# Giving one batch's feature sums a place of their own in the TensorE order, moving two GpSimd products to VectorE, and storing the last rows in two transfers instead of four

## The chip, the cores and the metric

The kernel runs on one core of a Trainium2 chip. Five engines work from instruction lists of their own: TensorE (PE in the profile; PEld is its weight loads), VectorE (DVE), ScalarE (ACT), GpSimd (POOL) and SyncE (SP, which here only issues transfers). An engine takes its list strictly in order, and waits at an instruction until the semaphores that it names have been raised by others. The metric is the device time of the program in microseconds, as the median of several runs. Before the change it is 265.54 us over 11 runs, from 265.09 to 267.2.

## The reference: what is computed

The first half is an attention without softmax over 4 batches, 4 heads, 1088 tokens and 32 channels per head. Every key and query is turned into 64 features, all products of two 8-number sketches:

```python
def phi(x):
    a = np.einsum('rd,bhsd->bhsr', S1, x)
    b = np.einsum('rd,bhsd->bhsr', S2, x)
    return np.einsum('bhsi,bhsj->bhsij', a, b).reshape(*x.shape[:-1], r * r)
q_p, k_p = (phi(q), phi(k))
kv = np.einsum('bhsf,bhsd->bhfd', k_p, v)
z = np.sum(k_p, axis=2)
num = np.einsum('bhsf,bhfd->bhsd', q_p, kv)
den = np.einsum('bhsf,bhf->bhs', q_p, z)[..., None] + 1e-06
return (num / den)
```

So each batch and head needs a 64 x 32 matrix `kv` and a vector `z` of 64 sums before its queries can be answered. The second half takes the 4352 rows of 128 numbers through `gelu(x @ w_in) @ w_out`, with 2048 hidden channels. The weights come as 64-bit floats; the kernel rounds them to 32 bits itself, out of their two 32-bit words.

## The kernel before, in words

**Tiles.** A batch's 1088 tokens are 1024 "main" tokens, worked in two chunks of 512 (eight chunks, n = 0 to 7), and 64 "remainder" tokens. The remainders of the four batches are chunk 8, of 256 tokens. The remainder's keys are worked in pairs: batches 0 and 2, and batches 1 and 3.

**The start.** Batch 0 is worked straight through, written out line by line from line 842. Keys are turned by TensorE, sketched, multiplied into features (line 383 by VectorE, line 380 by GpSimd) and multiplied with the values (`kv_first`, line 415). `key_features_rem(0, ..., by_pool=True)` (line 869) makes the remainder's features: ScalarE copies both sketches to SBUF (line 397) and GpSimd multiplies them (line 398). `kv_first_rem` (line 421) needs these; then ScalarE copies `kv` out (line 879), and the queries of chunk 0 are answered (line 625), divided (lines 640 to 646), turned (line 654) and given to the first hidden products (lines 688 and 673). Beside this the first two pieces of `w_in`, 256 columns each, are rounded (`class Rounding`): ScalarE scales the low words (line 260), VectorE takes the exponent field (line 264) and the mantissa field (line 266), ScalarE shifts the exponent (line 272), VectorE joins mantissa (line 280) and sign (line 285), and the last product (line 290) is GpSimd's for these two pieces. After the first of them GpSimd writes the gates of the `w_out` loads (line 180), and SyncE starts all further loads.

**The steps.** From line 911 on, the order is a list of steps t. Each step has one hidden product of 128 channels for a chunk (`hidden`, line 673), its GELU on ScalarE (line 680), then whatever was hung at that step with `at(t, ...)`, and then products with `w_out` (`project`, line 809, in the first steps; `two_products`, line 758, afterwards). Every instruction is tied to the one before it on its engine, so the order on each engine is the order of this text. Hidden results have two PSUM buffers.

**Batch 1's keys** (steps 14 to 23). VectorE turns the keys (line 352), spreads the features (lines 933 to 940), multiplies the remainder's (line 402), and adds over the tokens (`add_tokens`, lines 949 to 955), which leaves `k_s`, the partial sums for z. `finish_keys(1)` at step 21 does `kv_sum` on TensorE: 32 products for `kv` and 4 for its remainder (line 426), and then 4 products of `k_s` with ones for z, into the same PSUM bank beside `kv` (`part` 1). ScalarE copies 128 columns (line 444). At step 22 `turn_kv` turns `kv` (line 449), ScalarE copies it to `kz` (line 450), and VectorE folds z into the sketch of the queries (`sketch_of_z`, lines 475 to 478). `query_sketch(2)` at step 24 (line 560) needs that. Batches 2 and 3 go the same way at steps 45/46 and 77/78.

**The end.** Chunk 8's attention output is copied by ScalarE into `xT` (line 613), the two batches of a half side by side; two half results come from line 806, each for 128 tokens of two batches. `store` copies each to SBUF (line 815) and issues two transfers of 64 rows for it, one from SyncE's queue and one from ScalarE's (line 817).

## Time and profile before

| What | us |
|---|---|
| median of 11 runs | 265.54 |
| the profiled execution's own time | 265.54 |
| its span, first to last instruction | 263.8 |
| what lies around the span | 1.74 |
| TensorE busy in the span | 257.3 |
| VectorE, ScalarE, GpSimd busy | 150.5, 116.8, 165.9 |

The profiled execution has the time of the median, so sums made against it need no correction. "Busy" of TensorE counts a pipelined matmul to its modelled end. In the timeline each row gives start, duration, engine, line, operation, output and inputs, the count, and in brackets how long the engine was idle before it and who released it. Rows of one line are merged while they follow each other. The waits view has the same idle times summed: us in total, number, longest. TensorE's granted clock is at full speed in all stages before the last 2 us.

### The profile page before, as it was taken

The page shows a single profiled execution, that of the slowest core. Times are in us where ns is not written, and L with a number is a line of the kernel's source. Part 1 is how long each engine was busy: PE and PEld are TensorE (multiplying, and loading weights), DVE is VectorE, ACT ScalarE, POOL GpSimd, SP SyncE. Part 2 cuts the span into 40 slices and gives each one's busy share as a digit, 9 for nine tenths or more (in the row PEclk, how much of TensorE's full clock was granted, in tenths as well). Part 3 has the DMA queues.
Part 4 walks back from the last instruction along what each step waited for, and adds up shares of the span by engine and source line. Part 5 has one row for each costly group of instructions (what it writes and reads, how often), then busy time and mean ns, then how long its engine had stood idle before and what let it go on. Part 6 is the DMA issues. An engine that isn't in the chain of part 4 may idle for free.

```text
span 263.8 us, 5751 instructions
## 1 busy us (share of the span) xinstructions
PE 257.3 (98%) x2329; PEld 132.4 (50%) x2329; DVE 150.5 (57%) x305; ACT 116.8 (44%) x227; POOL 165.9 (63%) x175
## 2 busy tenths in 40 slices
PE   8999999979999999999999999999999999999994
PEld 6745444335454554444444454444445444445794
DVE  2886888958697996682176967560555032600240
ACT  4674777423625343353335333623453334433441
POOL 3614016779978775687767867777768776877200
PEclk9999999999999999999999999999999999999998
DMA  7479748710000201102000011001000100010020
GB/s 206 131 217 365 179 106 207 218 31 10 0 2 11 32 0 26 18 2 40 2 0 2 0 18 25 2 13 27 2 0 14 30 4 0 10 32 0 2 40 20
DMA packets 29562, 13.48 MB, mean 51 GB/s; under 512 B 21856, under 2 KB 27744, under 8 KB 29536
## 3 DMA queue, kind: packets, MB, share of 16 engines
q1 hardware_dynamic: 29344, 13.05, 19.8%
q8 instruction: 18, 0.29, 0.5%
q10 hardware_dynamic: 192, 0.07, 0.1%
q14 instruction: 8, 0.07, 0.1%
HBM read 10.88 MB, written 2.23 MB: 50 GB/s over the span
## 4 chain that ended last, share of the span: by engine, by line
PE 81%; DVE 6%; DMA 5%; SPq 5%; issue 1%; POOL 0%; ACT 0%; DVEq 0%
PE h_ps L673 37%; PE o_ps L758 33%; DMA block<-in_moe_w_out_dram 4%; PE w_ps L806 3%; DVE w_ps L949 1%; PE w_ps L609 1%; SPq L121 1%; PE w_ps L840 1%; SPq L132 1%; PE w_ps L560 1%; SPq L173 1%; PE w_ps L426 1%; DMA k<-in_k_dram 1%; DVE k_p L940 1%; PE h_ps L326 1%
## 5 line engine op out<-in xcount | busy, mean ns | idle before, releaser
L673 PE MATMUL h_ps<-xT,w_in 128*64 128x512 f32 (+3 forms) x516 | 138.7, 576 | 0.0
L680 ACT ACTIVATE block<-h_ps 128x512 f32<-128x512 f32 (+1 forms) x128 | 73.0, 570 | 120.7 <-PE h_ps L673 114.2
L758 PE MATMUL o_ps<-block,w_out 128*64 128x256 f32 x224 | 57.7, 380 | 0.0
L673 PEld LDWEIGHTS h_ps<-xT,w_in 128*64 128x64 f32 (+1 forms) x516 | 42.1, 143 | 30.1 <-issue 11.7
L723 POOL TENSOR_TENSOR bits_low<-block 128x512 f32<-128x512 f32 x28 | 35.6, 1273 | 29.8 <-ACT block L680 29.8
L758 PEld LDWEIGHTS o_ps<-block,w_out 128*64 128x64 f32 x224 | 30.2, 137 | 38.5 <-issue 25.8
L724 POOL TENSOR_TENSOR bits_a<-block 128x512 f32<-128x512 f32 x28 | 35.8, 1280 | 13.9 <-ACT block L680 13.9
L725 POOL TENSOR_TENSOR bits_e<-bits_a,block 128x512 f32<-128x512 f32 x28 | 36.2, 1294 | 2.2
L726 POOL TENSOR_TENSOR bits_m<-block,bits_e 128x512 f32<-128x512 f32 x28 | 35.8, 1279 | 2.2
L758 PE MATMUL o_ps<-block,small 128*64 128x256 f32 x112 | 29.1, 382 | 0.0
L758 PE MATMUL o_ps<-bits_low,small 128*64 128x256 f32 x112 | 29.1, 382 | 0.0
L758 PE MATMUL o_ps<-bits_a,small 128*64 128x256 f32 x112 | 29.0, 381 | 0.0
L774 DVE TENSOR_TENSOR sums<-o_ps,sums 64x512 f32<-64x512 f32 x8 | 5.5, 683 | 41.2 <-ACT sums L771 23.6
L758 PE MATMUL o_ps<-bits_m,w_out 128*64 128x256 f32 x112 | 28.7, 379 | 0.0
L572 DVE STREAM_TRANSPOSE w_ps<-w_ps 128x512 f32<-128x512 f32 (+1 forms) x7 | 4.8, 691 | 39.6 <-PE w_ps L560 39.6
L758 PEld LDWEIGHTS o_ps<-block,small 128*64 128x64 f32 x112 | 14.8, 137 | 19.0 <-issue 10.6
L758 PE MATMUL o_ps<-bits_e,small 128*64 128x256 f32 x112 | 17.1, 384 | 0.0
L809 PE MATMUL o_ps<-g,w_out 128*128 128x512 f32 x32 | 16.4, 600 | 0.1
L758 PEld LDWEIGHTS o_ps<-bits_m,w_out 128*64 128x64 f32 x112 | 15.3, 137 | 0.0
L758 PEld LDWEIGHTS o_ps<-bits_a,small 128*64 128x64 f32 x112 | 14.9, 137 | 0.0
L758 PEld LDWEIGHTS o_ps<-bits_low,small 128*64 128x64 f32 x112 | 14.8, 137 | 0.0
L758 PEld LDWEIGHTS o_ps<-bits_e,small 128*64 128x64 f32 x112 | 7.5, 136 | 10.6 <-issue 9.1
(181 smaller groups left out, 300.5 us busy)
## 6 DMA issues: line engine op xcount, KB each, us to landing
block<-in_moe_w_in_dram SPq DMA_DIRECT2D x3, 512.0 KB, 6.8
block<-in_moe_w_out_dram SPq DMA_DIRECT2D x3, 512.0 KB, 11.8
k<-in_k_dram SPq DMA_DIRECT2D x12, 128.0 KB, 2.7
v<-in_v_dram SPq DMA_DIRECT2D x12, 128.0 KB, 3.1
q<-in_q_dram SPq DMA_DIRECT2D x24, 64.0 KB, 2.1
out_dram<-oT SPq DMA_DIRECT2D x24, 64.0 KB, 2.2
k<-in_k_dram SPq DMA_DIRECT2D x2, 256.0 KB, 2.7
q<-in_q_dram SPq DMA_DIRECT2D x2, 256.0 KB, 3.8
```

The source lines that it names most:

```text
L121: sp.dma_start(out=q_sb[n][h * 32:(h + 1) * 32].rearrange("t x j d -> t (x j d)"), in_=q[n // NCH, h, at:at + CW, :].rearrange("(t n) d -> ...
L572: dve.transpose(out=tok, in_=ps[:, :, :H2])
L673: pe.matmul(ps[rows, :W], lhsT=w[:, rows], rhs=xT[n][:, :W], start=True, stop=True)
L680: act.activation(out=g_of[n, fi][:, :W], in_=ps[:, :W], func=ACT.Gelu)
L723: pool.tensor_sub(out=s[3], in0=a11, in1=a21)
L724: pool.tensor_add(out=s[1], in0=a21, in1=a22)
L725: pool.tensor_sub(out=s[2], in0=s[1], in1=a11)
L726: pool.tensor_sub(out=s[4], in0=a12, in1=s[2])
L758: pe.matmul(acc[n][bank][half * 64:(half + 1) * 64, col:col + HW], lhsT=fixed, rhs=moving, start=opens and e == 0 and name in "4715", stop ...
L774: dve.tensor_add(out=C[lo, 1], in0=a1[lo], in1=C[lo, 0])
L806: pe.matmul(o_of[n][i][:, :128], lhsT=g[:, i * 128:(i + 1) * 128], rhs=w_tile(w_out_sb, fi), start=first, stop=final)
L809: pe.matmul(o_of[n], lhsT=w_tile(w_out_sb, fi), rhs=g, start=first, stop=final)
```

## The change

Five edits.

1. `kv_sum` no longer does the four z products. A new `z_sum` does them, with a start of its own, and a new `fold_z` does the fold into the query sketch. For batch 1 the z products move from step 21 (right behind `kv`) to step 23, behind that step's hidden product; the fold moves from step 22 to step 23, behind them. For batches 2 and 3 the order on TensorE and VectorE stays as it was.
2. `take_kv` copies 64 columns and not 128.
3. The first remainder features (batches 0 and 2) are made as the second ones are: ScalarE copies one sketch, VectorE multiplies it with the other out of PSUM. They come ahead of the rounding of `w_in[0]` on VectorE, and GpSimd does nothing for them.
4. `w_in[1]`: its mantissa field (line 266) moves behind the divisions of chunk 0, and its last product moves from GpSimd to VectorE, ahead of the two products of `expand_multiply` (line 538).
5. Chunk 8's `xT` is written with the two batches of a half interleaved token by token (each ScalarE write steps over one element), so that a half's 128 rows go out in one transfer from SyncE; ScalarE issues none.

```diff
         def fields(self):
+            self.exponent_fields()
+            self.mantissa_fields()
...
-    def key_features_rem(pair, ps, by_pool=False):
+    def key_features_rem(pair, ps):
...
-        both = att.tile([128, H, 2 * R], FP, name="a_rem")
-        if by_pool:
-            act.copy(out=both, in_=ab)
-            pool.tensor_mul(**spread(k_p_rem[pair], both[:, :, 0:R], both[:, :, R:2 * R]))
-            return
-        a = both[:, :, 0:R]
+        a = att.tile([128, H, R], FP, name="a_rem")
         act.copy(out=a, in_=ab[:, :, 0:R])
         dve.tensor_mul(**spread(k_p_rem[pair], a, ab[:, :, R:2 * R]))
...
+    def z_sum(b):
+
+        ps = held["kv"][:, 0]
         for h in range(H):
-            kv_product(ps, ones, k_s[b][:, h], h, 1, stop=True)
+            kv_product(ps, ones, k_s[b][:, h], h, 1, start=True, stop=True)
+
+    def fold_z(b):
+        sketch_of_z(b, held["kv"][:, 0], F)
...
     def take_kv(b, ps):
-        kv_T[b] = att.tile([128, 128], FP, name="kv_T")
-        act.copy(out=kv_T[b], in_=ps[:, :128])
+        kv_T[b] = att.tile([128, F], FP, name="kv_T")
+        act.copy(out=kv_T[b], in_=ps[:, :F])
...
-            pe.matmul(banks[rows, 1, :128], lhsT=kv_T[b][:, :F], rhs=ident, start=True, stop=True)
+            pe.matmul(banks[rows, 1, :128], lhsT=kv_T[b], rhs=ident, start=True, stop=True)
         act.copy(out=kz[b], in_=banks[:, 1, :128])
-        sketch_of_z(b, banks[:, 0], F)
...
-        act.copy(out=xT[n][:, :W].rearrange("p (s x) -> p s x", s=2), in_=banks[:, :, :W // 2])
+        to = xT[n][:, :W]
+        to = to.rearrange("p (s x) -> p s x", s=2) if m == 1 else to.rearrange("p (s t i) -> p s i t", s=2, i=m)
+        act.copy(out=to, in_=banks[:, :, :W // 2] if m == 1 else banks[:, :, :W // 2].rearrange("p s (i t) -> p s i t", i=m))
...
-                for b, queue in ((i, sp), (i + 2, act)):
-                    queue.dma_start(out=out[b * S + MAIN:(b + 1) * S, :],
-                                    in_=oT[b // 2 * REM:(b // 2 + 1) * REM, i, :])
+                sp.dma_start(out=out.rearrange("(two b s) d -> two b s d", two=2, s=S)[:, i, MAIN:S, :].rearrange("two s d -> s two d"),
+                             in_=oT[:, i, :])
...
-    key_features_rem(0, banks[1], by_pool=True)
+    key_features_rem(0, banks[1])
...
-    w_in[1].fields()
+    w_in[1].exponent_fields()
...
     for banks, tokens in zip(nd, parts):
         divide(0, banks, tokens, by_head_pair=True)
+    w_in[1].mantissa_fields()
...
-    w_in[1].product(pool)
+    w_in[1].product()
...
-    def finish_keys(b):
+    def finish_keys(b, z=True):
         held["kv"] = work_banks()
         kv_sum(b, held["kv"][:, 0])
+        if z:
+            z_sum(b)
         take_kv(b, held["kv"][:, 0])
...
-    at(21, finish_keys, 1)
+    at(21, finish_keys, 1, False)
     at(22, lambda: turn_kv(1, held["kv"]))
+    at(23, z_sum, 1)
+    at(23, fold_z, 1)
     at(23, query_turn, 3)
...
             at(t + 14, lambda b=b: turn_kv(b, held["kv"]))
+            at(t + 14, fold_z, b)
```

## The prediction

> **What bounds the kernel now.** I first read the page's busy line: does one engine fill the span? TensorE does, with 257.3 of 263.8 us. What is left to win is therefore its own idle time, and the second view is the list of TensorE's waits over the whole span, longest first.

> ```profile
> PE 257.3 (98%) x2329; PEld 132.4 (50%) x2329; DVE 150.5 (57%) x305; ACT 116.8 (44%) x227; POOL 165.9 (63%) x175
> ```

> ```profile
> PE w_ps L426 <- DVE k_s L955: 1.6, 1, 1.6
> PE w_ps L840 <- PEq L1128: 0.8, 1, 0.8
> PE o_ps L421 <- POOL k_p_rem L398: 0.3, 1, 0.3
> PE h_ps L654 <- DVE x_tok L646: 0.2, 1, 0.2
> ```

> The whole list has four entries, and two are touched: the 1.6 us before batch 1's z products and the 0.3 us before the first remainder's. The third view is busy time by stage (columns: length, PE, PEld, DVE, ACT, POOL busy with counts, granted clock, DMA share, GB/s).

> ```profile
> 44.00:52.00 8.00, 8.00 (x43) 2.53 (x41) 7.90 (x10) 3.69 (x9) 6.62 (x10) 1.00 0.72 209
> 52.00:56.00 4.00, 2.42 (x86) 1.55 (x86) 2.83 (x3) 1.23 (x3) 3.25 (x3) 1.00 0.26 64
> 56.00:60.00 4.00, 4.00 (x42) 1.69 (x38) 1.34 (x4) 1.82 (x4) 2.94 (x3) 1.00 0.14 22
> 60.00:100.00 40.00, 40.00 (x388) 19.57 (x380) 34.81 (x59) 16.33 (x32) 32.63 (x37) 1.00 0.05 9
> ```

> VectorE fills 44 to 52 (7.90 of 8): it makes batch 1's keys, and TensorE runs into its end. Behind that, TensorE has no hole until the last 4 us, so a microsecond won at 53 is kept if nothing else turns late. Fourth, the timeline around the hole and around the start and end:

> ```profile
> 10.66 0.77 POOL L398 TENSOR_TENSOR k_p_rem<-a_rem 128x256 f32<-128x256 f32 x1 [0.82 <-ACT a_rem L397]
> 11.49 0.42 PE L421 MATMUL o_ps<-v_rem_aug,k_p_rem 128*64 128x33 f32 x8 [0.26 <-POOL k_p_rem L398]
> ...
> 17.59 0.30 PEld L673 LDWEIGHTS h_ps<-xT,w_in 128*128 128x128 f32 x2 [0.75 <-POOL w_in L290]
> ...
> 53.05 0.29 PE L426 MATMUL w_ps<-k_p_rem,v_rem_aug 128*32 128x64 f32 x8
> ...
> 54.46 0.42 DVE L955 TENSOR_TENSOR k_s<-w_ps,k_p_rem 64x256 f32<-64x256 f32 x1
> ...
> 54.93 0.32 PE L426 MATMUL w_ps<-k_s,ones 128*32 128x64 f32 x8 [1.58 <-DVE k_s L955]
> 55.18 1.08 PE L673 MATMUL h_ps<-xT,w_in 128*64 128x512 f32 x4
> ...
> 259.97 1.18 SPq L817 DMA_DIRECT2D out_dram<-oT  x2
> 259.97 1.44 ACTq L817 DMA_DIRECT2D out_dram<-oT  x2
> ```

> TensorE ends kv's remainder at 53.34, waits 1.58 for `k_s`, and two hidden products that need no `k_s` stand behind the wait.

> **Part 1, z at step 23.** After kv's remainder TensorE now goes on with step 22's hidden product. In the chain before, the hidden product behind small matmuls took 1.01, the turn of kv 0.22, the next hidden product 0.86: z comes up at 53.34 + 2.09 = 55.43. Two things must be ready. `k_s` ends at 54.88 and released TensorE at 54.93: 0.50 to spare. The new instruction also waits for ScalarE, up to the copy `kz`, which stands behind step 22's GELU; before, `kz` ended at 57.06, 1.88 after that hidden product began, so now at about 55.22: 0.2 to spare. ScalarE's own copy of kv no longer waits for z (53.34 instead of 55.25), and a hidden buffer is free, as step 21's GELU ended by 52.96. Behind z on TensorE stand step 23's `w_out` products and step 24's hidden product; a late z would hold them. z's eight records take 0.22 in batch 2, where they follow without a hole; the products behind them took 1.01 there where 0.86 is usual, so 0.15 goes back. Old start of those products: 57.33. New: 55.43 + 0.22 + 0.15 = 55.80, a gain of 1.53; the bare hole is 1.58. I take 1.55. Bounds: 1.85 without any refill time (hole, 0.10 less on z, 0.15 less on the hidden product, rounded up), 0.8 if z waits for a VectorE that slips by 1.2 (below).

> What is late next? The fold on VectorE took 57.09 to 57.85. It would now run from about 55.8 to 56.6; the query sketch (line 560) comes up at 55.80 + 1.30 + 0.86 = 57.96, so 1.3 to spare. The turn of chunk 3's queries behind the fold (0.71) moves along. GpSimd's sums of the next block waited 1.56 for a GELU at 56.98; they can now follow the previous ones at 55.41. Cost: nothing.

> **Part 2, the narrower copy.** 0.27 each, three times, shorter by some hundredths; TensorE has a hidden product (0.86) between copy and turn. Nothing, and nothing if that cover went.

> **Part 3, the first remainder features.** GpSimd's 0.77 goes. VectorE is free of `q_pT` at 10.54, and ScalarE's copy ends at 10.58. The same product on VectorE took 0.41 (line 402, same shape, one input from PSUM): about 10.62 to 11.03. TensorE ends `kv_first` at 11.23 and goes straight on: 0.26 won. The price lies behind it on VectorE: the fields of `w_in[0]`, formerly 10.46 to 10.96, start at about 11.03. ScalarE's line 272 waits for the first of them and stands ahead of the copy of kv (line 879): 11.03 + 0.29, then 0.50 is 11.85, then 0.22 is 12.07. TensorE has the query turns (0.57 up to the next start) after line 421 and wants kv at 12.18. So 0.1 to spare; if the product takes 0.7, the gain falls to 0.1. Line 285 ends at about 12.3, not 12.05, GpSimd's product of `w_in[0]` moves 0.24 later, and with it the gates on POOL's queue and every later load on SyncE's. Those have room: the 512 KB blocks of `w_out` landed in a median of 11.8, so the first, issued at 15.54, near 27.3, and VectorE read it at 28.73; GpSimd's copy of the remainder values ended 3.4 before its next work. On the other side VectorE loses what stood beside GpSimd: line 280 took 0.66 beside line 398 where 0.42 is usual, line 266 took 0.83 beside line 290 where 0.29 is usual.

> **Part 4, `w_in[1]`.** Line 266 leaves the stretch before the divisions and falls into VectorE's 0.59 hole before 15.64, where it fits with 0.29. The product needs 0.42 on VectorE (line 290 for `w_out[0]`) after line 285 and its 0.42, instead of 0.73 on GpSimd and a handover: ready at 17.15, not 17.54. The hidden product that needs it stood at 17.59, and the six records there took 2.92 where six steps of 0.43 are 2.58 and 0.16 is usual run-out: 0.18 was waiting. The next limit is the GELU that frees the buffer, so I take 0.10. `expand_multiply` moves to 18.1 from 17.92; its reader starts at 19.5, or 19.15 now. `w_out[0]` follows and is read at 20.2. Parts 3 and 4 together: 0.36, between -0.1 (all of it eaten, w_in[0] late) and 0.7 (the 0.2 of line 654 and the rest of the 0.3 also go).

> **Part 5, the end.** Before, the last two transfers were issued at 260.65; SyncE's issue took 0.51 to 0.53, ScalarE's 0.55 and 0.77; landing took 1.8 and 2.1 (medians). Now one of 64 KB from SyncE: 64 KB stores landed in a median of 2.2, 64 KB query loads in 2.1, with issues of 0.42 to 0.63. Against ScalarE's 0.77 and 2.1 I take 0.10 won, between 0.3 won (SyncE's 1.8 stays) and 0.9 lost (the slowest landing of any store, 3.0). The first transfer's issue ends before the second copy is done, so nothing queues. The interleaved copy (line 613) has 0.06 to spare before TensorE's hidden product at 241.94. The nearest row for a step of 8 bytes is line 260's reading, 0.43 against 0.37 for a plain 128x256 copy: 0.00 to 0.07, I take 0.03 lost.

> [...]

> **Sum.** 265.54 - 1.55 - 0.36 - 0.10 + 0.03 = 263.56; I say 263.5, as the bounds of parts 1 and 3 reach further down than the refill I charged.

> **Rivals.**
> - Only the middle pays (12 in 100): ScalarE's order eats the start, the end is even. 265.54 - 1.55 = 264.0. For it: 0.1 to spare at kv's copy. Against: VectorE gets back 0.78 of time lost beside GpSimd.
> - The wait comes back at z (10 in 100): VectorE's key stage is full, and 0.24 later loads or GpSimd's neighbourhood (line 285 took 0.94 at 44.67 against 0.69) may shift `k_s`. From 0.5 late on it costs; 1.2 late leaves 0.8 of part 1: 264.3. If nothing of it were won and the start paid: 265.1. Against: VectorE's chain there starts from ScalarE work that TensorE paces, so it moves forward with the start.
> - More than the sum (8 in 100): the start gives 0.7, the end 0.3, the refills vanish: 262.7.
> - Slower (4 in 100): VectorE becomes the bound between 60 and 103, where it is 87% busy. Its two-input sums took 0.41 or 1.42 (lines 792, 793) by what GpSimd did beside them, and the fold of batch 2 at 102.0 has 0.84 before TensorE's line 560 at 102.86. A shifted phase adds 1.0 per hit; it decides from 0.84 + 2.0 = 2.8 late, three hits. Four would give 263.5 + 4.0 - 0.84 = 266.7. Against: two of the three sums there are already the slow kind.
> - The forecast itself: 66 in 100, with a range of 263.1 to 263.9.

> **Range and chances.** 262.8 to 264.6 takes in the forecast, the middle alone, the wait half back and most of the better case; outside lie the slow case and parts of the others. A measurement of this kernel tells 0.2% (0.5 us) from no change. Faster: all but the slow case and the worst of the returning wait, 92; within 0.2%: 4; slower: 4.

> **What would show it.** Right: no TensorE wait for `k_s`, z products about 2.1 us after kv's remainder, line 560 of batch 1 some 1.9 earlier than 59.42; line 421 without a wait and near 11.23; no PEld wait for GpSimd's `w_in`; one SyncE issue per half and a similar tail after the last copy. Wrong: a wait of TensorE for ScalarE's kv copy near 12.2, for `kz` or `k_s` near 55, a new hole near 100, or a tail over 3.5 us from the last copy to the end.

## The result and the profile after

The changed kernel takes 264.22 us, the median of 15 runs (263.75 to 265.24), against 265.47 us over 57 runs of the kernel before on the same chip: a ratio of 0.9953, with a 95% interval of 0.9941 to 0.9964. That is 1.25 us less. The prediction was 263.5 us, 2.0 less than the profiled execution of before: the sign is right, the time lies inside the range, and about 0.7 us of the gain is missing. Of all executions told of here, one, of the kernel "early and one" below, ran in a slower state of the chip (272.01 us at a granted clock of 0.95), and it is left out of every comparison.

The profiled execution of the changed kernel took 265.24 us (span 263.5), the longest of its runs, so its span is not compared with the other; places in it are. First the busy line of its page and the list of TensorE's waits over the whole span (what it waited for, us in total, times, longest):

```profile
PE 257.6 (98%) x2329; PEld 132.5 (50%) x2329; DVE 151.2 (57%) x307; ACT 116.8 (44%) x227; POOL 163.5 (62%) x173
```

```profile
PE w_ps L849 <- PEq L1143: 0.8, 1, 0.8
PE h_ps L635 <- issue: 0.5, 1, 0.5
PE o_ps L819 <- DVE w_out L297: 0.5, 1, 0.5
PE o_ps L768 <- DVE sums L789: 0.3, 1, 0.3
PE h_ps L664 <- DVE x_tok L656: 0.2, 1, 0.2
```

The two entries that the prediction counted on are gone: the 1.6 for `k_s` and the 0.3 for the remainder's features. Three have come: 0.5 inside the 64 products of line 635 (the query answers, 625 before), 0.5 for VectorE's last product of the second `w_out` piece (297, 290 before), and 0.3 near 199 us for VectorE's sums. None was in the prediction.

The busy time by stage, in the columns and windows of the prediction:

```profile
44.00:52.00 8.00, 8.00 (x41) 2.72 (x42) 7.83 (x11) 3.94 (x8) 6.61 (x10) 1.00 0.75 207
52.00:56.00 4.00, 4.00 (x90) 1.95 (x88) 3.69 (x4) 2.51 (x6) 3.84 (x4) 1.00 0.32 88
56.00:60.00 4.00, 4.00 (x48) 1.87 (x48) 1.78 (x5) 1.23 (x3) 3.92 (x4) 1.00 0.12 19
60.00:100.00 40.00, 40.00 (x392) 19.56 (x390) 34.97 (x60) 16.59 (x32) 31.89 (x37) 1.00 0.06 10
```

From 52 to 56 TensorE is now busy for 4.00 of 4.00, where it was 2.42. Behind that nothing has opened up to 100. The timeline shows how (start, length, engine and line; line 428 is kv and z, 683 the hidden product, 458 kv's turn, 459 ScalarE's copy `kz`, 965 VectorE's last step of `k_s`):

```profile
53.92 0.29 PE L428 MATMUL w_ps<-k_p_rem,v_rem_aug 128*32 128x64 f32 x8
...
54.15 1.08 PE L683 MATMUL h_ps<-xT,w_in 128*64 128x512 f32 x4
...
55.06 0.39 PE L458 MATMUL w_ps<-ident,kv_T 128*64 128x128 f32 x4
...
55.36 0.42 DVE L965 TENSOR_TENSOR k_s<-w_ps,k_p_rem 64x256 f32<-64x256 f32 x1
55.77 0.26 ACT L459 COPY kz<-w_ps 128x128 f32<-128x128 f32 x1
56.23 0.16 PEld L428 LDWEIGHTS w_ps<-k_s,ones 128*32 128x32 f32 x8 [0.81 <-ACT kz L459]
56.24 0.32 PE L428 MATMUL w_ps<-k_s,ones 128*32 128x64 f32 x8
```

z comes 2.03 behind the end of kv's remainder (54.21), where 2.09 was worked out; `k_s` is ready at 55.78, 0.46 before z, where 0.50 was. `kz` ends at 56.03, 0.2 before z, as said. The weight loads' 0.81 idle before `kz` costs nothing, as the matmuls have no gap.

At the end there is one issue per half, the second copy goes on beside the first issue, and from the start of that copy to the end of the span it is 3.40 (before 3.44, from its copy at 260.32):

```profile
259.71 1.29 SPq L826 DMA_DIRECT2D out_dram<-oT  x2
260.06 0.29 DVE L825 COPY oT<-w_ps 128x128 f32<-128x128 f32 x1 [0.38 <-PE w_ps L816]
```

To put the whole together I timed TensorE's own list in stages, between the same instructions in every profile: from the first query products (the 16th record of line 534, 7.8 us in before) to the end. That leaves out how early the first loads came in: the start of the list lies between 7.43 and 7.96 in these five. Three more executions stand beside the two that are compared; they are told of below.

```
us from ... to                          before  after  again  one more  one fewer
query products .. tokens turned (664)     7.39   7.88   7.36      7.36       7.00
.. step 4's output products (819)         7.93   8.23   8.24      7.85       7.85
.. batch 1's query sketch (568)          36.32  34.81  34.81     34.81      34.81
.. 192 us                               132.71 132.71 132.71    132.71     132.72
.. 204 us                                11.90  12.26  12.26     11.91      11.91
.. last product                          55.96  55.98  55.96     55.98      55.98
.. end of the span                        3.75   3.71   3.72      3.71       3.71
```

The middle gives 1.51 in each of the four. The rest is a matter of three places: the first row, which varies; the second, 0.3 worse where 0.1 better was expected; and the row to 204, 0.35 worse.

### The profile page after: what moved, and what is told of

It is laid out like the page before. It is cut to its first block, busy times and chain, and to the rows that moved or that the text cites. A ratio compares the mean times of both kernels' runs of the same rounds, so it can differ in the third digit from the quotient of the medians.

```text
span 263.5 us, 5749 instructions
## 1 busy us (share of the span) xinstructions
PE 257.6 (98%) x2329; PEld 132.5 (50%) x2329; DVE 151.2 (57%) x307; ACT 116.8 (44%) x227; POOL 163.5 (62%) x173
## 4 chain that ended last, share of the span: by engine, by line
PE 93%; DVE 3%; issue 1%; POOL 1%; ACT 0%; DVEq 0%
PE h_ps L683 43%; PE o_ps L768 33%; PE o_ps L819 5%; PE w_ps L816 3%; PE w_ps L617 1%; PE w_ps L428 1%; PE w_ps L849 1%; PE w_ps L568 1%; PE o_ps L417 1%; PE h_ps L333 1%; PE w_ps L935 1%; DVE q_pT L546 0%; PE w_ps L534 0%; DVE x_tok L656 0%; PE h_ps L635 0%
## 5 line engine op out<-in xcount | busy, mean ns | idle before, releaser
L690 ACT ACTIVATE g<-h_ps 128x512 f32<-128x512 f32 x16 | 9.5, 596 | 7.7 <-PE h_ps L683 7.2
```

The source lines that it names most:

```text
L690: act.activation(out=g_of[n, fi][:, :W], in_=ps[:, :W], func=ACT.Gelu)
```

## The experiments

Each was run in five rounds beside the kernel before on the same chip, so each has its own ratio to it.

**First the parts.** At this point the profile after was all there was, and its largest new entry the stand inside line 635. Theory A: TensorE's own supply of instructions fails there now and then. Theory B: the new order makes that hole in every execution. Theory C: the gain of the middle is given back later. The changed kernel was run again, and three kernels with some of its parts. The edits are the diff of the change, cut into its parts:

```diff
 e1_again:      all of it
 e2_z_only:     parts 1 and 2 (z_sum, fold_z, the narrower kv_T)
 e3_start_only: parts 3 and 4 (key_features_rem on VectorE; w_in[1])
 e4_end_only:   part 5 (one transfer per half, the interleaved xT copy)
```

> The changed kernel once more, for a second profiled execution. In the first one TensorE was 0.19 us ahead at 12.25, then stood still inside the 64 products of line 635 until 13.37 with nothing that released it, and VectorE's last product for w_out[1] came 0.5 late at 23.42; the middle gave 1.50. Theory A (the stand-still is TensorE's own supply of instructions, which comes when it comes, and varies from execution to execution): the hole of line 635 is smaller or gone or elsewhere in this execution, the span is shorter by what it lost, and times between 263.7 and 265.2 again. Theory B (the new order itself makes it, in every execution): the same hole of 0.8 at the same place and the same late product at 23.4. Median against before: 0.994 to 0.997.

> Of the change only z_sum and fold_z at step 23 and the narrower copy. Start and end as before. Prediction's part 1: 1.5 us less than before (ratio 0.994, about 264.0), the hole at line 428 gone and z some 2.1 behind kv's remainder. Theory A: this alone is as fast as the whole change or a little faster, as the start edits give nothing. Theory C (the middle's gain is given back later, through a new wait near the drains): the ratio is 0.996 or more and TensorE has new waits behind 60.

> Only parts 3 and 4: first remainder features and w_in[1]'s product by VectorE, its mantissa field later. The prediction had 0.36 us less (ratio 0.9986). Theory A: no wait at the remainder's products, 0.2 ahead at 12.2, then some of it lost where TensorE runs out of instructions: ratio 0.998 to 1.001, with the hole before batch 1's z products still 1.5 to 1.9. Theory B: 0.4 to 0.8 us more than before (ratio 1.0015 to 1.003).

> Only part 5: interleaved xT, one transfer per half. The prediction had 0.07 us less. All theories: between 0.2 less and 0.3 more (ratio 0.999 to 1.001); the copy of xT in 0.37 to 0.44, the time from the last VectorE copy to the end 3.2 before, 3.0 to 3.3 here.

Measured: again 264.13 us (ratio 0.9957, 0.9943 to 0.9972); z alone 263.99 (0.9945, 0.9926 to 0.9965); the start alone 265.51 (1.0002, 0.9989 to 1.0015); the end alone 265.23 (1.0002, 0.9984 to 1.0021).

So z alone gives as much as the whole change, and the two start edits together give nothing. Theory B falls for the stand inside line 635, which is in neither of the two other profiles with the start edits, as theory A has it. C falls too: z alone keeps 1.4. The other half of B holds, the late product of `w_out[1]`: all three profiles so far with both start edits have 0.51 to 0.53 of waiting for line 297, and no profile without them shows it.

**What holds line 297?** In the profile after, five rows tell it:

```profile
22.49 0.41 DVE L292 SCALAR_TENSOR_TENSOR bits_e<-small,bits_r 128x256 uint32<-128x256 uint32 x1
...
22.87 0.60 PE L664 MATMUL w_ps<-ident,x_tok 128*128 128x128 f32 x4
...
23.14 0.24 POOL L476 TENSOR_TENSOR S_ab<-sT,own_r 128x32 f32<-128x32 f32 x1
...
23.42 0.42 DVE L297 TENSOR_TENSOR w_out<-bits_m,bits_e 128x256 f32<-128x256 f32 x1 [0.52 <-POOL S_ab L476]
...
23.99 1.10 PE L819 MATMUL o_ps<-g,w_out 128*128 128x512 f32 x2 [0.52 <-DVE w_out L297]
```

VectorE ends the signs (292) at 22.90 and stands idle for 0.52 with everything ready, while GpSimd works through the eight small instructions of `spread_sketches`. In before, signs and product stand close together, with the same instructions of GpSimd beside them:

```profile
22.01 0.41 DVE L285 SCALAR_TENSOR_TENSOR bits_e<-small,bits_r 128x256 uint32<-128x256 uint32 x1
22.53 0.45 DVE L290 TENSOR_TENSOR w_out<-bits_m,bits_e 128x256 f32<-128x256 f32 x1
```

In the changed kernel the profile names one of GpSimd's as the releaser. My theory D was that GpSimd's small instructions keep VectorE out. Two kernels try it, one by moving these instructions to 13 us, one also without part 4; and two take parts 3 and 4 alone:

```diff
 e5_early_spread (the changed kernel), e8_all_but_win (parts 1, 2, 3, 5)
     load_rest()
+    spread_sketches()
...
-    at(11, spread_sketches)
 e6_features_only: part 3 alone        e7_win_only: part 4 alone
```

> The changed kernel with GpSimd's eight small instructions of `spread_sketches` (own_r, S_abc, S_ab; 22.30 to 24.12 in its profile) issued right behind the gates of the last loads, so at about 13.3, where GpSimd stands idle for 8.31 us. Theory D (VectorE's last product for w_out[1], line 297, is locked out by these small instructions because the w_out chain comes 0.2 later by one more product on VectorE): VectorE's 0.52 idle before that product goes, TensorE's 0.5 before step 4's output products goes down to the 0.0 to 0.2 that ScalarE's copy of xT leaves, and the time is 0.3 to 0.5 below the changed kernel: 263.6 to 263.85, ratio to before 0.993 to 0.994. Rival E (that wait only covers another one of the same length, or GpSimd's instructions now hold VectorE up at 13 to 15 in the divisions): 264.1 to 264.4, the wait moves to another place before 25 us.

> Part 3 alone (the remainder's first key features by VectorE, w_in[1] left as before). Theory D: nothing is added to VectorE behind 12 us, so the w_out chain is not later, line 297 comes before GpSimd's small instructions as in the kernel before, and the gain at the remainder's products is kept: 0.2 to 0.3 less than before, 265.15 to 265.25, ratio 0.999. Rival F (the gain at 11 us is eaten before 23 us whatever stands there, by ScalarE or by the divisions): 265.4, ratio 1.000, with a new or longer wait of TensorE between 12 and 24.

> Part 4 alone (w_in[1]'s mantissa fields behind the divisions, its product on VectorE; the remainder's features on GpSimd as before). Theory D: the w_out chain on VectorE is some 0.2 to 0.3 later, line 297 of w_out[1] is locked out by GpSimd's small instructions, and TensorE waits 0.5 for it near 23.5: 0.3 to 0.5 slower than before, 265.75 to 265.95, ratio 1.0015. Rival F: the product is ready 0.3 to 0.4 earlier and nothing else moves: 265.3 to 265.45, ratio 0.9995 to 1.000.

> Parts 1, 2, 3 and 5 without part 4 (w_in[1] by GpSimd as before), and with `spread_sketches` at 13 us as in the run with it early. Theory D: the sum of what each part gives without the lock-out: the middle 1.45, the first features 0.25, the end 0.05 to 0.1, so 263.6 to 263.75, ratio 0.993 to 0.9935, below the changed kernel (264.15) and z alone (264.0). Rival F (the start gives nothing in any form): 263.9 to 264.0, as z and the end alone would.

Measured: early 263.68 (0.9928, 0.9907 to 0.9950); part 3 alone 265.56 (0.9996, 0.9975 to 1.0018); part 4 alone 265.33 (0.9997, 0.9974 to 1.0020); all but part 4 264.14 (0.9939, 0.9914 to 0.9964). The time of the first is what D foretold, and D is wrong all the same. The profile of that kernel has no GpSimd instruction between 21.1 and 22.0, and the stand is there, to the hundredth:

```profile
21.08 0.41 DVE L292 SCALAR_TENSOR_TENSOR bits_e<-small,bits_r 128x256 uint32<-128x256 uint32 x1
...
22.02 0.42 DVE L297 TENSOR_TENSOR w_out<-bits_m,bits_e 128x256 f32<-128x256 f32 x1 [0.52 <-DVE bits_e L292]
```

What had gone was the 0.3 near 199, 175 us after anything that the edit touches. D's other three numbers were missed too. Part 4 alone does not lock line 297 out, and part 3 alone gains nothing.

**Theory G: the place in the list.** I then numbered VectorE's instructions in each trace, its first one as number 0 and semaphore waits included (of the changed kernel's 378 records, 68 are such bare waits, 0.02 to 0.05 us each, which the timeline does not print; none of the other 310 names more than one semaphore). In all profiles so far I looked for instructions that start at least 0.25 us after VectorE was free and after everything they wait for was done. (Where `S_ab` is named as the releaser, this is what hides it: later GpSimd work raises the same semaphore again, but the product needs only GpSimd's sum of line 285, done at 22.35.) They are these:

```
kernel                     number   instruction                    idle   just ahead of it
after, again               63       w_out[1]'s product (297)       0.52   bare wait
start only, early spread   63       w_out[1]'s product (297)       0.51, 0.52   bare wait
part 4 alone               191      S_abc of batch 2 (485)         0.47   bare wait
after, again               319      sums, first of line 786        0.46   bare wait
```

63, 191 and 319 are 128 apart. In the kernels that show no stand, the same numbers fall on an instruction that follows work of 0.17 us or more (number 63 in before is the third `w_in` piece's mantissa field, behind 0.66; with part 4 alone a copy, behind the product's 0.45; and so on). Among the transfers there are 8 KB ones of the kind "instruction", though the profile does not tell for which engine; in the changed kernel one of them begins at 198.25, 1.1 after VectorE passed number 318. So the reading, from these spacings alone, is that VectorE's list is to be counted in blocks of 128, that the first of a block is some 0.46 late, and that this is hidden when VectorE still has work in hand and shows when the instruction ahead is a mere wait that ended after the engine had run dry (number 62 in the changed kernel ends at 22.96, 0.06 behind the signs). The change adds two products and a wait to VectorE's list ahead of 22 us and so moves the product of `w_out[1]` from number 60 to 63; part 3 alone moves it to 61, part 4 alone to 62. The early spread takes two waits out further on, so that line 786 has numbers 317 and 318 there: that is where its 0.3 went. What makes the first of a block late is not shown. It is not a transfer of that moment: in the changed kernel none of the 8 KB ones begins between the start of the span and 28.5, and the stand before number 63 ends at 23.42. How the list reaches the engine is not shown either.

G says that numbers alone decide, so three kernels change nothing but the numbers: one more VectorE instruction ahead of everything (an initial fill done twice, 0.09 us where VectorE is idle), one fewer, and three more in the kernel before, which put its own line 290 on number 63. A fourth adds the one to the kernel with the early spread.

```diff
 e9_one_more (changed kernel), e10_three_in_before (kernel before: range(4)), e11_early_and_one
-    dve.memset(ones, 1.0)
+    for _ in range(2):
+        dve.memset(ones, 1.0)
 e12_one_fewer (changed kernel)
-    dve.memset(ones, 1.0)
+    pool.memset(ones, 1.0)
```

> The changed kernel with one more VectorE instruction at its very start: `ones` is set twice (0.09 us, at 0.8 us, where VectorE then idles for 2.6). Nothing else differs. Theory G: VectorE gets its instructions in blocks of 128; counting every one that the trace records, waits on semaphores included, its numbers 63, 191 and 319 each open a block and come some 0.46 after the one before, unless VectorE is still busy with earlier work. The stands of 0.52 before `w_out[1]`'s product (number 63) and of 0.46 before line 786 near 197 (number 319), each just behind a semaphore wait, are that. One more instruction puts number 63 on the semaphore wait ahead of the product, beside the signs' 0.41, and 319 on the wait ahead of line 786, beside line 784's 0.68: both stands go, TensorE's waits of 0.5 at line 819 and 0.3 at line 768 with them, 0.6 to 0.8 less than the changed kernel: 263.35 to 263.6. Theory D (the product is held up by what GpSimd or the data do): nothing changes, 264.1 to 264.3, the stand stays before the same product.

> The kernel before, without any part of the change, with three more VectorE instructions at its start (`ones` set four times). Theory G: number 63 is now the product for `w_out[1]` (line 290 of before), right behind its semaphore wait, so the 0.5 stand and TensorE's 0.5 wait near 23.1 appear in the kernel before: 0.3 to 0.5 slower, 265.75 to 265.95, ratio 1.001 to 1.002; nothing else moves. Theory D: three memsets at 0.8 us cost nothing, 265.4 to 265.5, no stand.

> The changed kernel with `spread_sketches` at 13 us (263.68 in its own run, where the 0.52 stand before `w_out[1]`'s product was left and that at line 786 was gone) and one more VectorE instruction at the start. Theory G: the first stand goes too, 0.3 to 0.5 less: 263.2 to 263.4, the fastest of all, ratio 0.991 to 0.992. Theory D: 263.6 to 263.75, as without the extra instruction.

> The changed kernel with one VectorE instruction fewer at its start: `ones` is set by GpSimd instead. Theory G: number 63 is now the copy of xT behind `w_out[1]`'s product and number 319 the second instruction of line 786, both behind work of 0.42, and 191 is a semaphore wait behind 0.23 of work; none stands behind a bare wait, so the two stands and TensorE's waits of 0.5 and 0.3 go as with one instruction more: 263.3 to 263.65, ratio 0.992 to 0.993. Theory H (it was the extra memset's own effect on the first microseconds that helped, not the numbers): 264.1 to 264.3, the stands stay.

Measured: one more 263.47 (0.9924, 0.9912 to 0.9936); one fewer 263.71 (0.9941, 0.9920 to 0.9961, a wide interval; 0.06 above G's 263.3 to 263.65); three in before 265.87 (1.0011, 1.0002 to 1.0019); early and one 263.36 over five runs (0.9929, 0.9915 to 0.9944). With one more, product and signs stand close together and TensorE has no wait there:

```profile
21.52 0.41 DVE L293 SCALAR_TENSOR_TENSOR bits_e<-small,bits_r 128x256 uint32<-128x256 uint32 x1
22.04 0.45 DVE L298 TENSOR_TENSOR w_out<-bits_m,bits_e 128x256 f32<-128x256 f32 x1
...
22.64 0.67 PE L820 MATMUL o_ps<-g,w_out 128*128 128x512 f32 x1
```

With three more in the kernel before, which holds no part of the change, the stand appears in it, and TensorE's wait with it:

```profile
22.22 0.47 DVE L286 SCALAR_TENSOR_TENSOR bits_e<-small,bits_r 128x256 uint32<-128x256 uint32 x1
23.21 0.43 DVE L291 TENSOR_TENSOR w_out<-bits_m,bits_e 128x256 f32<-128x256 f32 x1 [0.52 <-POOL S_abc L471]
...
23.78 0.67 PE L810 MATMUL o_ps<-g,w_out 128*128 128x512 f32 x1 [0.58 <-DVE w_out L291]
```

The hole near 199 goes the same way. First the changed kernel, where line 786 is number 319, then the one with one more, where its wait is:

```profile
196.45 0.68 DVE L784 TENSOR_TENSOR sums<-o_ps,sums 64x512 f32<-64x512 f32 x1 [3.12 <-PE h_ps L683]
...
197.59 0.85 DVE L786 TENSOR_TENSOR sums<-o_ps,sums 64x256 f32<-64x256 f32 x2 [0.46 <-ACT block L690]
```

```profile
195.10 0.68 DVE L785 TENSOR_TENSOR sums<-o_ps,sums 64x512 f32<-64x512 f32 x1 [3.12 <-PE h_ps L684]
...
195.89 0.85 DVE L787 TENSOR_TENSOR sums<-o_ps,sums 64x256 f32<-64x256 f32 x2
```

So what G says of the numbers is shown for VectorE, from both sides: the stands go with one instruction more and with one fewer, and the one at number 63 (0.52) appears in the kernel before with three. In time, the two are worth 0.39 (8.24 to 7.85) and 0.35 (12.26 to 11.91) in the table. The kernel with one more is faster by 0.7 us than the change and by 2.0 than before; its interval does not tell it from the early spread, early and one, or one fewer. Its two waits were named with a total of 0.6 to 0.8, and it is 0.66 to 0.75 faster than the change. "Early and one" lies inside G's 263.2 to 263.4, but its ratio not inside G's 0.991 to 0.992; with its interval, some 263.3 to 264.0, it tells no difference from one more alone, which fits an early spread that does nothing by itself.

**Why the first row of the table varies.** With both start edits and no stand in line 635, tokens are turned either 7.00 to 7.03 (start only, early spread, one fewer) or 7.36 (again, one more) behind the first query products; without either 7.36 to 7.39, and with part 4 alone 7.19. Three profiles show what decides. In "one fewer", the second piece of `w_in` landed at 10.36, its exponent field (268) slips in ahead of GpSimd's product, and the denominators (650) wait only for TensorE:

```profile
12.31 0.29 DVE L268 TENSOR_SCALAR bits_e<-small 128x256 uint32<-128x256 uint32 x1
...
12.48 0.73 POOL L297 TENSOR_TENSOR w_in<-bits_m,bits_e 128x256 f32<-128x256 f32 x1 [2.47 <-DVE bits_e L292]
...
12.93 0.23 DVE L650 TENSOR_SCALAR den_tok<-h_ps 128x4 f32<-128x4 f32 x2 [0.33 <-PE h_ps L635]
```

In "one more", it landed at 12.23. VectorE waits 0.37 for it, meets GpSimd's product, and takes 0.60 instead of 0.29; TensorE's wait for `x_tok` grows from 0.20 to 0.49:

```profile
11.97 0.73 POOL L298 TENSOR_TENSOR w_in<-bits_m,bits_e 128x256 f32<-128x256 f32 x1 [2.40 <-DVE bits_e L293]
...
12.26 0.60 DVE L269 TENSOR_SCALAR bits_e<-small 128x256 uint32<-128x256 uint32 x1 [0.37 <-DMA small<-in_moe_w_in_dram]
...
14.79 0.41 PE L665 MATMUL h_ps<-ident,x_tok 128*128 128x128 f32 x2 [0.49 <-DVE x_tok L657]
```

And in "part 3 alone", where the mantissa field (266) still stands ahead of the divisions, it is that which meets GpSimd's product, and the gain of part 3 ends there in both profiles that have it without part 4 (7.35, and 7.37 in all but part 4):

```profile
11.95 0.73 POOL L290 TENSOR_TENSOR w_in<-bits_m,bits_e 128x256 f32<-128x256 f32 x1 [2.47 <-DVE bits_e L285]
11.99 0.85 DVE L266 TENSOR_SCALAR bits_a<-small 128x256 uint32<-128x256 uint32 x1
```

In the last two, GpSimd's product begins first and VectorE's instruction ends 0.16 after it (12.86 and 12.70, 12.84 and 12.68), having taken 0.60 and 0.85. In the first, VectorE begins first, by 0.17, and takes 0.29; GpSimd's product begins 0.12 before VectorE's end and takes 0.73, as in the other two. What holds VectorE up beside GpSimd is not shown.

So part 3 pays only with part 4, which takes the mantissa field out of the way, and only if the second piece of `w_in` has landed when GpSimd's product of the first begins (11.86 to 12.72 in the six profiles with both edits). Over thirteen profiles it landed between 10.24 and 12.55, and in two of the six, too late. The 7.19 of part 4 alone fits: GpSimd's product of the remainder's features took 0.63 there instead of before's 0.77, TensorE had no wait of 0.15 or more for it, and with the mantissa field out of the way those 0.2 came through. In z alone and three in before that product took 0.63 as well, without such a wait, but the mantissa field stands in the way and the row is 7.36.

**What stays open.** The stand in line 635 (0.52 idle, at 12.84, inside one run of 64 like products with all their inputs ready) was seen once in six profiles with both start edits. Among the transfers of the kind "instruction" there are also 16 KB ones, whose engine the profile does not tell either; the first of them behind the start began at 11.04 in that profile and between 9.08 and 10.38 in twelve others. That the stand has to do with them was my guess from one profile; it is not shown and was not tried.

## Why the prediction was right or wrong

**Part 1, z (1.55; measured 1.51).** Right, in size and in its steps: z 2.03 behind kv's remainder (2.09 worked out), `k_s` 0.46 ahead (0.50), `kz` 0.2 ahead, no wait at z, and the query sketch of batch 1 at 58.79 instead of 59.42 although TensorE came 0.87 late into the stage in that execution (the prediction's sign of being right, 1.9 earlier than 59.42, counted the start's gain too; it is 1.81 in "one fewer"). Nothing of it was given back up to 192 us, and the rivals "the wait comes back at z" and "slower", which put holes at z or between 60 and 103, have no row for them.

**Part 2 (nothing).** Right: ScalarE's copy of kv takes 0.21 instead of 0.27, and the hidden product covers it.

**Part 3 (0.26, 0.1 to spare at ScalarE's copy of kv).** The wait at the remainder's products is gone in every profile with part 3; in "one fewer" the stage to the turned tokens is 0.39 shorter. The step that failed is the one that looked for what is late next: I named ScalarE's copy of kv, where no profile has a wait. Late was VectorE itself, at the exponent field of `w_in[1]`, because the piece may not have landed. In before it landed at 10.75 and was read at 11.98; I did not look at that 1.2 of room, and the landing moves by 2.3 from execution to execution. So the term is 0.0 or 0.37, not 0.26. And the 0.26 was itself not in every execution without part 3: before and the end alone have it (0.26 and 0.28, GpSimd's product 0.77 and 0.79), while z alone, part 4 alone and three in before have no wait of 0.15 or more there (0.63).

**Part 4 (0.10).** Right in size: from the turned tokens to the same hidden product behind them TensorE takes 3.27 or 3.28 in every profile compared that holds part 4, and 3.37 in all others. But the prediction treated its two pieces as gains of 0.1 beside part 3; moving the mantissa field was what let part 3 pay at all, as part 3 alone shows.

**"`w_out[0]` follows and is read at 20.2."** Here the sum failed. I followed the chain of roundings to `w_out[0]` and not to `w_out[1]`, 2 us later, nor further; and no following of waits would have shown the stand, since nothing in before has it. Two more products and a wait in VectorE's list gave the product of `w_out[1]` number 63 instead of 60, and everything behind it another number too. The two stands cost 0.39 and 0.35, 0.74 together, as much as the gap between 263.5 and the 264.2 measured. With them taken out by one idle instruction, the same change takes 263.47. That the sum then fits is in part chance: summed over the table's rows, "one more", where `w_in[1]` landed too late, is 1.63 below before, and "one fewer", where it landed in time, 1.98, while their medians lie 2.06 and 1.73 below before's; the rest lies ahead of the first query products and in what varies from execution to execution. The rival "only the middle pays" came close to the time (264.0) for a reason that was not the one it gave.

**Part 5 (0.10 won, 0.03 lost).** The interleaved copy took 0.39 instead of 0.37, and the table shows 0.02 or nothing for it; the tail is 0.04 shorter, not 0.10. About nothing in all, as the end alone says (265.23, no difference within its interval). With SyncE as the only issuer, the two issues took 0.61 and 0.58 (0.51 to 0.53 before), and the first held nothing up: it ended at 260.31, the second copy at 260.35, and the second issue began at 260.41.

**Chances and range.** 0.47% faster is inside "faster", and 264.2 inside 262.8 to 264.6, but outside the forecast's own 263.1 to 263.9, to which it gave 66 in 100. It is inside the range because that was made wide for other losses; of the stands the prediction had nothing.

## What to carry to other kernels

When a change adds or removes instructions on VectorE, the one engine for which this is shown here, count where its blocks of instructions begin (at numbers 63, 191 and 319 here), and see that none begins right behind a bare semaphore wait on a path that sets the time; where one does, an idle instruction far ahead moves it, and here that was worth 0.66 to 0.75 us, where the whole change had won 1.25. Before crediting a gain to what was edited, take the parts apart: a part can depend on another, and a run that hits the predicted number can do so for another reason, as the early spread did. Room in front of a transfer is only as much as its earliest and latest landing over several executions leave (10.24 and 12.55 for `w_in`'s second piece here).
